# One Trainium2 core: a layer of sliding attention and a gated feed-forward, with the order of its steps replaced

## Chip, core and metric

The kernel runs on one core of one Trainium2 chip. The metric is the device time of one execution in microseconds (us), as the median of several runs. Engines are named as the profile names them: PE is TensorE, DVE is VectorE, ACT is ScalarE, POOL is GpSimd and SP is SyncE, which here only starts transfers.

## What is computed

Two blocks follow each other on 2048 tokens of 512 values in bfloat16. The first is attention with 32 heads of 16 values, in which each token looks at itself and seven earlier ones, two apart. The second is a gated feed-forward of width 1376. Each has a layer norm ahead of it and its input added behind it.

```python
def _A_ref(x, wqkv, wo):                      # H = 32, Dh = 16, W = 8, dil = 2
    qkv = (x @ wqkv).reshape(B, S, 3, H, Dh).transpose(2, 0, 3, 1, 4)
    q, k, v = qkv[0], qkv[1], qkv[2]
    idx = pos[:, None] - (jnp.arange(W) * dil)[None, :]
    mask = idx >= 0
    logits = jnp.einsum("bhsd,bhswd->bhsw", q, kg) * Dh ** -0.5   # kg, vg: k, v gathered at idx
    attn = softmax(jnp.where(mask, logits, -1e9))
    o = jnp.einsum("bhsw,bhswd->bhsd", attn, vg)
    return o.transpose(0, 2, 1, 3).reshape(B, S, D) @ wo

def _B_ref(x, W_gate, W_up, W_down):
    gate = x @ W_gate
    return ((gate * (gate > 0)) * (x @ W_up)) @ W_down

h = x + _A_ref(_layernorm(x), A_wqkv, A_wo)
out = h + _B_ref(_layernorm(h), B_W_gate, B_W_up, B_W_down)
```

## The kernel before

The tokens are cut into four chunks of 512 (tk 0 to 3 in the code, here the first to the fourth chunk). Each chunk goes through the same steps, and the chunks overlap:

- Layer norm: statistics on DVE (L467, L470), the scale on ACT (L480, L484), the normalised rows into a tile "row" (L515 on DVE, L512 on ACT). The rows are then transposed into a "quad" tile, either on PE (L544) with a copy out by ACT or DVE (L558, L560), or by DMA transposes that SP starts (L533).
- Query, key and value projections on PE (L585) and copies out by ACT (L593). In the first chunk the projections are cut into small column pieces, so that PE can begin when the first 128 tokens are normalised.
- Scores: DVE multiplies the query by shifted keys (L636, L651), in one case pairs are added, and PE sums over a head's values with a 32 column selection matrix (L642, L694). ACT takes the exponential (L708), PE sums it per head (L725), ACT inverts that, and DVE scales the exponentials (L752).
- The weights are then broadcast over a head's values by DMA, from tile "ex" into tile "big" (L768), four transfers of 128 KB for each half of the window, started by SP or by POOL.
- DVE multiplies them by the shifted values (L800). The eight products are summed by an accumulating DMA of 512 KB that POOL starts (L843), and the rest by DVE (L803, L837).
- Output projection on PE (L881). DVE adds the input (L892), ACT squares for the second norm (L457), DVE writes the centred rows (L510), and SP transposes them by DMA (L533).
- Gate and up on PE (L954; the last 96 columns at L921). ACT copies them out, into tile "up_sb" (L958) and tile "gr" (L961), and DVE multiplies them into "gT" (L982). There are two up_sb buffers.
- Down projection on PE (L1005). For the third and fourth chunk DVE scales it and adds the residual (L1013), and SP stores it (L1019). For the first and second chunk ACT scales it into up_sb (L1011), POOL adds that to x_sm by an accumulating DMA (L1034), and SP stores x_sm (L1037). Until that addition has landed the up_sb buffer is not free.

All results of PE go into eight "bank" tiles.

What sets the order is a list of numbers. The code first writes down all steps (add, class Plan), with the engine, what each depends on, what buffers it takes, and a duration and latency for the planner. RANK gives every step a place. With RANK the planner takes the steps strictly by it and gives each the buffer that by its own reckoning comes free first; each engine then has its steps in that order, and runs them strictly one after another. Only this line of it matters here:

```python
            for op in (waiting[-1:] if RANK else waiting):
```

Constants such as SW, PEL, AL and DL are the planner's latencies. They issue nothing. The first steps (setup) are not in the list: the loads of the input and of the attention weights, the load of the gate weights, and the constants.

Of the kernel before, what the change touches and what calls it, by code (L numbers as in the profile page):

```python
# [8 lines left out]
P = 128  # L9
# [192 lines left out]
def kernel(  # L202
# [103 lines left out]
    def f_load(n, i):  # L306
        if n == "d":
            lo, hi = (0, 5) if i == 0 else (5, NFF)
            nc.sync.dma_start(
                wd_sb[:, lo:hi, :], B_W_down[lo * P:hi * P, :].rearrange("(ft p) n -> p ft n", p=P))  # L310
            if FTAIL and i:
                nc.sync.dma_start(wd_sb[:FTAIL, NFF, :], B_W_down[NFF * P:F, :])
        else:
            w = B_W_up.rearrange("(dt p) f -> p dt f", p=P)
            nc.sync.dma_start(wgu_sb[:, 2 * i:2 * i + 2, 1, :], w[:, 2 * i:2 * i + 2, :])

    def setup():
# [31 lines left out]
        nc.sync.dma_start(wgu_sb[:, :, 0, :], B_W_gate.rearrange("(dt p) f -> p dt f", p=P))  # L349

# [40 lines left out]

    BCN = 4
# [4 lines left out]
    TMT = (0, 1, 2, 3)  # L397
    TTM, DTG, ATE = 0.0825, 0.27, 0.225
# [6 lines left out]
    SW = 0.21  # L405
    PEL = 0.22
    A5, A10, AX, AS = 0.48, 0.9, 0.713, 0.2
    AL = 0.13
    D2, D5, D10, D20, D40, DST, DSM = 0.335, 0.665, 0.603, 1.135, 2.202, 0.595, 0.08
    DXN = 0.33  # L410
    DL = 0.12
# [18 lines left out]
    fills = [add(("warm", 0), "PE", 5.6, f_warm, [], -500, take=[wb])]  # L430

# [8 lines left out]
    def layernorm(tk, src, dst_slots, pr, groups, on_act, residual=None):  # L440
# [7 lines left out]
        for grp in groups:  # L448
# [78 lines left out]
            for j0 in range(lo, hi, step):  # L527
# [24 lines left out]
                tev = not residual and tk == 0 and j0 == 1  # L552
# [15 lines left out]
    for tk in range(NCK):  # L568
# [52 lines left out]
        kp = {t: kdone.get((tk - 1, t)) for t in range(NT)}  # L621
        for hf in range(2):
# [55 lines left out]
            elif (tk, hf) in PRE:  # L678
# [19 lines left out]
                scd = [add(("sc%d" % hf, tk), "PE", nu * MM + SW, f_sc, [a], apr, take=[sc], use=[prd[0][1]], lat=PEL)]  # L698
# [8 lines left out]
            def f_ex(sc=sc, ex=ex):  # L707
                nc.scalar.activation(out=ex.t[:], in_=sc.t[:], func=ACT.Exp, scale=SCALE)  # L708

            def f_mk(hf=hf, ex=ex):  # L710
                V.tensor_tensor(out=ex.t[:, 0:PADL], in0=ex.t[:, 0:PADL], in1=mask[:, hf, :],
                                op=ALU.mult)

            a = add(("ex%d" % hf, tk), "ACT", A5, f_ex, scd, apr, take=[ex], use=[sc], lat=AL)
            if tk == 0:
                a = add(("mk%d" % hf, tk), "DVE", DSM, f_mk, [a], apr, use=[ex], lat=DL)
            exs.append(ex)
            exd.append(a)


        dn, rc = Buf(at_s), Buf(rc_s)

        def f_dn(exs=exs, dn=dn, tk=tk, es=None):
# [371 lines left out]
```

## Time and profile before

| what | value |
|---|---|
| three runs | 191.80, 192.64 and 192.98 us; median 192.64 us |
| span of the profiled execution, from first to last instruction | 190.2 us |
| granted TensorE clock, mean | 0.998 |
| HBM read, written | 8.42 MB, 2.10 MB |

The profile is of one execution. Its page gives the span; a time of that execution beside the span is not given, and the median of the runs is 2.4 us above the span. Times in the profile count from the span's first instruction. A row of the grouped view has line, engine, operation, output and input tiles, shapes and count, then busy time, mean ns of one, and idle time before. A row of the timeline has start, length, engine, line, operation, tiles and count, and in brackets the engine's idle time before it with what ended that. SPq is SP's queue; its length there is the time to start the transfers, not to move them.

### The profile page before, as it was taken

Reading aid. Unit: us, or ns where it says so; the run is one execution under the profiler, and the core shown is the slowest. Engines: PE = TensorE matmul, PEld = TensorE weight load, DVE = VectorE, ACT = ScalarE, POOL = GpSimd, SP = SyncE. Lnnn points to the kernel's source line nnn. Section 1 sums busy time; section 2 is a strip of 40 time slices with the busy share of each in tenths; the row PEclk is TensorE's granted clock in tenths of the full one; section 3 lists DMA queues with packets and bytes.
Section 4 is the critical chain, followed back from the end, with each engine's and each line's share of the span. In section 5 each row is a group of like instructions: output and inputs, shape, how many; then the busy total and the mean of one; then the engine's idle time right before and its main releaser. Section 6 shows DMA issues by size and latency. Waiting matters only on the chain.

```text
span 190.2 us, 3080 instructions
## 1 busy us (share of the span) xinstructions
PE 185.1 (97%) x1127; PEld 95.4 (50%) x1127; DVE 150.7 (79%) x231; ACT 113.5 (60%) x234; POOL 25.2 (13%) x47
## 2 busy tenths in 40 slices
PE   7799999999999999999999999999999999999993
PEld 7676555554444445544344464444454444455453
DVE  5899999999999999999999998998485712114324
ACT  2579999985467945762483795146466713358500
POOL 4000221400000004230033123027000000000000
PEclk9999999999999999999999999999999999999999
DMA  5999364993198858998438798779922211000503
GB/s 182 281 347 370 90 163 87 191 194 59 21 330 177 233 166 153 194 191 182 83 65 152 142 181 186 180 137 166 221 44 55 55 28 59 28 0 0 165 3 110
DMA packets 27743, 26.98 MB, mean 142 GB/s; under 512 B 14704, under 2 KB 23248, under 8 KB 27728
## 3 DMA queue, kind: packets, MB, share of 16 engines
q1 hardware_dynamic: 23696, 15.34, 29.7%
q0 software_dynamic: 3312, 10.49, 28.6%
q10 hardware_dynamic: 720, 0.95, 1.5%
q8 instruction: 9, 0.15, 0.3%
q14 instruction: 6, 0.05, 0.1%
HBM read 8.42 MB, written 2.10 MB: 55 GB/s over the span
## 4 chain that ended last, share of the span: by engine, by line
PE 82%; ACT 11%; DMA 3%; DVE 1%; issue 1%; SPq 0%
PE bank L954 37%; PE bank L1005 20%; PE bank L585 12%; PE bank L881 7%; ACT row L512 5%; DMA x_sm<-in_A_x_dram 3%; PE bank L921 3%; ACT quad L560 2%; ACT vT L593 2%; PE bank L642 2%; ACT quad L593 1%; PE bank L694 1%; ACT kT L593 1%; ACT ex L708 1%; SPq L323 0%
## 5 line engine op out<-in xcount | busy, mean ns | idle before, releaser
L954 PE MATMUL bank<-quad,wgu_sb 128*128 128x512 bf16 x320 | 72.3, 379 | 0.0
L954 PEld LDWEIGHTS <-wgu_sb 128*128 128x128 bf16 x320 | 30.9, 98 | 37.3 <-issue 1.7
L1005 PE MATMUL bank<-wd_sb,gT 128*128 128x512 bf16 (+3 forms) x198 | 39.7, 355 | 0.0
L958 ACT CAST up_sb<-bank 128x512 bf16<-128x512 f32 x40 | 23.1, 591 | 21.0 <-PE bank L954 14.9
L585 PE MATMUL bank<-quad,wqk_sb 128*128 128x512 bf16 (+2 forms) x176 | 30.4, 321 | 0.5 <-DVE quad L558 0.4
L961 ACT ACTIVATE gr<-bank 128x512 bf16<-128x512 f32 x40 | 23.3, 606 | 9.7 <-PE bank L954 8.2
L1005 PEld LDWEIGHTS <-gT 128*128 128x128 bf16 (+1 forms) x198 | 18.5, 98 | 19.7
L982 DVE TENSOR_TENSOR gT<-gr,up_sb 128x1024 bf16<-128x1024 bf16 x20 | 13.6, 686 | 14.4 <-PE bank L1005 7.0
L636 DVE TENSOR_TENSOR big<-quad,kT 128x4096 bf16<-128x4096 bf16 x11 | 24.8, 2279 | 0.0
L585 PEld LDWEIGHTS <-wqk_sb 128*128 128x128 bf16 x176 | 17.1, 113 | 11.4 <-issue 1.1
L800 DVE TENSOR_TENSOR big<-big,vT 128x4096 bf16<-128x4096 bf16 x9 | 20.4, 2281 | 0.0
L843 POOL DMA_DIRECT2D big<-big x13 | 11.6, 965 | 64.3 <-PE bank L954 32.6
L1013 DVE SCALAR_TENSOR_TENSOR row<-bank,iv,x_sm 128x512 bf16<-128x512 f32 (+2 forms) x10 | 6.3, 643 | 13.4 <-PE bank L1005 13.2
L457 ACT ACTIVATE junk<-x_sm,sm 128x512 bf16<-128x512 bf16 x16 | 11.6, 727 | 8.8 <-DVE x_sm L892 8.8
L585 PE MATMUL bank<-quad,wv_sb 128*128 128x512 bf16 x64 | 16.1, 380 | 0.2 <-ACT quad L560 0.2
L881 PE MATMUL bank<-wo_sb,quad 128*128 128x512 bf16 x64 | 15.0, 379 | 0.0
L892 DVE SCALAR_TENSOR_TENSOR x_sm<-x_sm,bank 128x512 bf16<-128x512 bf16 x16 | 10.8, 678 | 2.4 <-PE bank L881 2.4
L803 DVE TENSOR_TENSOR big<-big 128x1024 bf16<-128x1024 bf16 (+1 forms) x17 | 10.3, 622 | 1.6 <-DMA big<-big 1.4
L467 DVE BATCH_NORM_STATS2 st<-x_sm 128x6 f32<-128x512 bf16 x16 | 10.2, 679 | 1.1 <-DMA x_sm<-in_A_x_dram 1.1
L593 ACT CAST quad<-bank 128x512 bf16<-128x512 f32 x16 | 9.3, 594 | 2.5 <-PE bank L585 2.4
L593 ACT CAST kT<-bank 128x512 bf16<-128x512 f32 x16 | 9.3, 596 | 1.9 <-PE bank L585 1.0
L593 ACT CAST vT<-bank 128x512 bf16<-128x512 f32 x16 | 9.1, 610 | 2.1 <-PE bank L585 2.1
(80 smaller groups left out, 175.6 us busy)
## 6 DMA issues: line engine op xcount, KB each, us to landing
big<-big POOLq DMA_DIRECT2D x13, 512.0 KB, 5.2
big<-ex SPq DMA_DIRECT2D x20, 128.0 KB, 3.1
big<-ex POOLq DMA_DIRECT2D x12, 128.0 KB, 3.8
wgu_sb<-in_B_W_gate_dram SPq DMA_DIRECT2D x1, 1376.0 KB, 9.3
wgu_sb<-in_B_W_up_dram SPq DMA_DIRECT2D x2, 688.0 KB, 5.0
wd_sb<-in_B_W_down_dram SPq DMA_DIRECT2D x2, 640.0 KB, 5.7
x_sm<-in_A_x_dram SPq DMA_DIRECT2D x2, 512.0 KB, 6.2
wqk_sb<-wqk_sb POOLq DMA_DIRECT2D x2, 512.0 KB, 5.8
```

What stands on the lines that cost most here:

```text
L457: nc.scalar.activation(out=junk[:, j % 2, :], in_=h.t[:] if h else x_sm[:, tk * BPC + j, :], func=ACT.Square, bias=sm.t[:, j:j + 1], scale ...
L585: nc.tensor.matmul(mm.t[:, lo:hi], lhsT=wv_sb[:, dt, t:D:NT] if c == 2 else wqk_sb[:, dt, c * D + t:(c + 1) * D:NT], rhs=xnT.t[:, dt, lo:h ...
L593: nc.scalar.copy(out=o, in_=mm.t[:])
L636: V.tensor_tensor(out=pb.t[:].rearrange("p (t w) s -> p t w s", t=2), in0=q4, in1=k4, op=ALU.mult)
L800: V.tensor_tensor(out=mt.t[:], in0=ab.t[:], in1=v8, op=ALU.mult)
L843: nc.gpsimd.dma_start(mt.t[:, 0:4, :], mt.t[:, 4:8, :], accum_op=ALU.add)
L881: nc.tensor.matmul(od.t[:], lhsT=OT.t[:, t, j * P:(j + 1) * P], rhs=wo_sb[:, t, :], start=(t == 0), stop=(t == NT - 1 and tk not in RPE))
L954: nc.tensor.matmul(mm.t[:fs, lo:hi], lhsT=wgu_sb[:, dt, g, ft * P: ft * P + fs], rhs=hnT.t[:, dt, lo:hi], start=(dt == 0), stop=(dt == NT ...
L958: nc.scalar.copy(out=ub.t[:fs, i, :], in_=um.t[:fs, :])
L961: nc.scalar.activation(out=gr.t[:fs, i, :], in_=gm.t[:fs, :], func=ACT.Relu)
L982: V.tensor_tensor(out=gt.t[:fs, 0:n, :], in0=gr.t[:fs, 0:n, :], in1=ub.t[:fs, 0:n, :], op=ALU.mult)
L1005: nc.tensor.matmul(od.t[:, c0:c1], lhsT=gts[ft].t[:fs, ft % 2, j * P:(j + 1) * P], rhs=wd_sb[:fs, ft, c0:c1], start=(ft == 0), stop=(ft == ...
```

## The change

The table RANK is replaced by another one of the same 745 numbers. Of the old and the new one the first row:

```diff
 RANK = [
-    0, 1, 2, 3, 4, 5, 6, 7, 8, 9, 18, 10, 11, 12, 14, 15, 16, 17, 13, 19,
...
+    1, 0, 2, 4, 5, 6, 8, 9, 11, 12, 10, 7, 3, 13, 14, 15, 16, 17, 18, 21,
...
 ]
```

Four planner latencies change, and three switches are added, each at the value that keeps the program's steps as they were: MS is empty, TEV holds the tile that was written out before, and the gate weights would be loaded later only if LATE, which stays "ud", held a "g".

```diff
+        elif n == "g":
+            nc.sync.dma_start(wgu_sb[:, :, 0, :], B_W_gate.rearrange("(dt p) f -> p dt f", p=P))
...
-        nc.sync.dma_start(wgu_sb[:, :, 0, :], B_W_gate.rearrange("(dt p) f -> p dt f", p=P))
-
+        if "g" not in LATE:
+            f_load("g", 0)
...
+    MS = ()
...
+    TEV = (1,)
...
-    SW = 0.21
-    PEL = 0.22
+    SW = 0.19
+    PEL = 0.15
...
-    AL = 0.13
+    AL = 0.1
...
-    DL = 0.12
+    DL = 0.1
...
-                tev = not residual and tk == 0 and j0 == 1
+                tev = not residual and tk == 0 and j0 in TEV
...
-                scd = [add(("sc%d" % hf, tk), "PE", nu * MM + SW, f_sc, [a], apr, take=[sc], use=[prd[0][1]], lat=PEL)]
+                if tk in MS:
+                    both.append((sc, ex, [a], [prd[0][1]], nu, f_sc))
+                else:
+                    scd = [add(("sc%d" % hf, tk), "PE", nu * MM + SW, f_sc, [a], apr, take=[sc], use=[prd[0][1]], lat=PEL)]
+            elif tk in MS:
+                both.append((sc, ex, [a for a, _, _ in prd], [b for _, b, _ in prd], 4, lambda p=prd: [f() for _, _, f in p]))
...
-            for n in LATE:
+            for n in LATE.replace("g", ""):
```

Every engine has the same instructions in another order. In what follows a row is the line, the operation, the tile written and the tiles read (the number behind a name tells tiles of one kind apart), the shape and the count. Lines after the change are 2 to 23 higher: L475 was L467, L523 was L515, L566 was L558, L775 was L752, L791 was L768, L541 was L533, L963 was L940, L1057 was L1034, L866 was L843.

The first place is DVE's start: statistics (BN_STATS, BN_AGGR) of the first chunk's four row tiles, their normalised rows row_104 to row_107, and the copy of one transposed tile into quad. Before:

```order
L467 BN_STATS st_114<-x_sm 128x6
L470 BN_AGGR mv_117<-st_114 128x2
L515 TENSOR_SCALAR row_104<-x_sm,mv_117,rs_129 128x512
L467 BN_STATS st_115<-x_sm 128x6
L515 TENSOR_SCALAR row_105<-x_sm,mv_117,rs_129 128x512
L470 BN_AGGR mv_117<-st_115 128x2
L467 BN_STATS st_116<-x_sm 128x6
L470 BN_AGGR mv_117<-st_116 128x2
L558 COPY quad_79<-bank_140 128x4x128
L515 TENSOR_SCALAR row_106<-x_sm,mv_117,rs_129 128x512
```

After the change:

```order
L475 BN_STATS st_114<-x_sm 128x6
L478 BN_AGGR mv_117<-st_114 128x2
L523 TENSOR_SCALAR row_104<-x_sm,mv_117,rs_129 128x512
L475 BN_STATS st_115<-x_sm 128x6
L523 TENSOR_SCALAR row_105<-x_sm,mv_117,rs_129 128x512
L478 BN_AGGR mv_117<-st_115 128x2
L566 COPY quad_79<-bank_139 128x4x128
L475 BN_STATS st_116<-x_sm 128x6
L478 BN_AGGR mv_117<-st_116 128x2
L523 TENSOR_SCALAR row_106<-x_sm,mv_117,rs_129 128x512
```

The copy has moved ahead of the fourth tile's statistics. The first two tiles have also changed places: row_104 now holds the second 128 tokens, which the copy belongs to, and row_105 the first.

The second place is where the third chunk's attention ends and the fourth chunk's weights (ex_100 and ex_102) are scaled. On DVE before:

```order
L752 TENSOR_TENSOR ex_102<-ex_102,rec_103 128x512
L803 TENSOR_TENSOR wqk_sb<-wqk_sb 128x1024
L931 TENSOR_TENSOR row_108<-gr_112,bank_142 128x2x96
L837 TENSOR_TENSOR quad_83<-big_90 128x512
L837 TENSOR_TENSOR quad_83<-wqk_sb 128x512
L803 TENSOR_TENSOR big_89<-big_89 128x1024
L837 TENSOR_TENSOR quad_83<-big_89 128x512
```

After:

```order
L826 TENSOR_TENSOR wqk_sb<-wqk_sb 128x1024
L775 TENSOR_TENSOR ex_100<-ex_100,rec_103 128x512
L860 TENSOR_TENSOR quad_82<-wqk_sb 128x512
L826 TENSOR_TENSOR big_91<-big_91 128x1024
L860 TENSOR_TENSOR quad_82<-big_91 128x512
L775 TENSOR_TENSOR ex_102<-ex_102,rec_103 128x512
L915 SCALAR_TENSOR_TENSOR x_sm,sm_121<-x_sm,bank_141 128x512
```

The scaling of ex_102 has moved behind the last of the attention's output rows (quad). On SP, at the same place, the broadcast that reads ex_102 and the transposes of the third chunk's normalised rows (into quad_86), before:

```order
L768 DMA big_88<-ex_102 128x1x512 x4
L1037 DMA out_dram<-x_sm 128x2x512
L940 DMA_TRANSPOSE gT_97<-row_108 128x4x128
L533 DMA_TRANSPOSE quad_86<-row_107 128x4x128
L533 DMA_TRANSPOSE quad_86<-row_104 128x4x128
L533 DMA_TRANSPOSE quad_86<-row_105 128x4x128
L533 DMA_TRANSPOSE quad_86<-row_106 128x4x128
```

After:

```order
L963 DMA_TRANSPOSE gT_96<-row_108 128x4x128
L791 DMA big_89<-ex_102 128x1x512 x4
L541 DMA_TRANSPOSE quad_86<-row_104 128x4x128
L541 DMA_TRANSPOSE quad_86<-row_106 128x4x128
L541 DMA_TRANSPOSE quad_86<-row_105 128x4x128
L541 DMA_TRANSPOSE quad_86<-row_107 128x4x128
```

A store has gone from between them and the transpose of the second chunk's last feed-forward columns (gT) now stands ahead of the broadcast.

The third place is POOL's list around the first chunk's residual additions (x_sm from up_sb) and the third chunk's accumulations (big, wqk_sb). Before:

```order
L768 DMA big_91<-ex_102 128x1x512 x4
L1034 DMA x_sm<-up_sb_109 128x1024
L1034 DMA x_sm<-up_sb_110 128x1024
L843 DMA big_92<-big_92 128x2048
L843 DMA wqk_sb<-wqk_sb 128x2048
L843 DMA big_90<-big_90 128x2048
L843 DMA big_89<-big_89 128x2048
```

After:

```order
L791 DMA big_92<-ex_101 128x1x512 x4
L1057 DMA x_sm<-up_sb_110 128x1024
L866 DMA big_90<-big_90 128x2048
L866 DMA big_88<-big_88 128x2048
L1057 DMA x_sm<-up_sb_109 128x1024
L866 DMA wqk_sb<-wqk_sb 128x2048
L866 DMA big_91<-big_91 128x2048
```

Two accumulations now stand between the two additions.

More of the change, by code (lines that the diff above doesn't have):

```diff
@@ L430 @@
     fills = [add(("warm", 0), "PE", 5.6, f_warm, [], -500, take=[wb])]
+    if "g" in LATE:
+        wload["g"].append(add(("ldg", 0), "SP", 0.45, lambda: f_load("g", 0), wload["o"], 0, lat=1.0, dq=(1.0, 3.6)))
     def fill(d, k):
@@ L621 @@
         kp = {t: kdone.get((tk - 1, t)) for t in range(NT)}
+        both = []
         for hf in range(2):
@@ L705, with f_ex, f_mk @@
                                    take=[sc], use=[pb], lat=PEL))
[L707 to L718, printed above, removed]
+            if tk in MS and hf == 0:
+                continue
+            if tk in MS:
+                a = add(("sc1", tk), "PE", sum(x[4] for x in both) * MM + SW, lambda p=both: [x[5]() for x in p],
+                        [d for x in both for d in x[2]], apr, take=[x[0] for x in both], use=[d for x in both for d in x[3]], lat=PEL)
+                scs = [(h, x[0], x[1], [a]) for h, x in enumerate(both)]
+            else:
+                scs = [(hf, sc, ex, scd)]
+            for h, sc, ex, scd in scs:
+                def f_ex(sc=sc, ex=ex):
+                    nc.scalar.activation(out=ex.t[:], in_=sc.t[:], func=ACT.Exp, scale=SCALE)
+                def f_mk(h=h, ex=ex):
+                    V.tensor_tensor(out=ex.t[:, 0:PADL], in0=ex.t[:, 0:PADL], in1=mask[:, h, :],
+                                    op=ALU.mult)
+                a = add(("ex%d" % h, tk), "ACT", A5, f_ex, scd, apr, take=[ex], use=[sc], lat=AL)
+                if tk == 0:
+                    a = add(("mk%d" % h, tk), "DVE", DSM, f_mk, [a], apr, use=[ex], lat=DL)
+                exs.append(ex)
+                exd.append(a)
         dn, rc = Buf(at_s), Buf(rc_s)
```

74 rows, old and new, of the table RANK are left out of this document.

## The prediction

> **What bounds the kernel now.** I read the page's first two parts, then the busy time by stretches, what TensorE waited for, and the chain of waits. Part 1 of the page, with busy time and share of the span:
>
> ```profile
> span 190.2 us, 3080 instructions
> PE 185.1 (97%) x1127; PEld 95.4 (50%) x1127; DVE 150.7 (79%) x231; ACT 113.5 (60%) x234; POOL 25.2 (13%) x47
> ```
>
> TensorE (PE) is idle 190.2 - 185.1 = 5.1 us. The stretches say where (start:end, length, then each engine's busy time):
>
> ```profile
> 0.00:10.50 10.50, 8.48 (x128) 7.75 (x129) 7.82 (x29) 4.89 (x12) 1.91 (x16) 1.00 0.76 234
> 10.50:40.00 29.50, 29.34 (x210) 17.30 (x210) 29.27 (x48) 27.88 (x52) 5.90 (x8) 1.00 0.75 204
> 40.00:70.00 30.00, 30.00 (x180) 13.82 (x178) 30.00 (x36) 19.49 (x40) 0.00 (x0) 1.00 0.69 176
> ...
> 187.30:190.20 2.90, 0.00 (x0) 0.00 (x0) 0.35 (x1) 0.00 (x0) 0.00 (x0) 0.89 0.34 97
> ```
>
> About 2.0 us lie before 10.5, 0.2 before 40, 2.9 in the tail. TensorE's waits (total, times, longest) are all of the first two:
>
> ```profile
> PE bank L428 <- DVE warm L327: 1.0, 1, 1.0
> PE bank L544 <- DVE row L515: 0.5, 1, 0.5
> PE bank L585 <- DVE quad L558: 0.4, 1, 0.4
> PE bank L585 <- ACT quad L560: 0.2, 1, 0.2
> ```
>
> The 1.0 us stands before the first matmul of all, behind a memset in the setup, which the change leaves alone. The tail is the last output slice's arithmetic and store. So waits that another order can take away sum to 0.5 + 0.4 + 0.2 = 1.1 us. Is busy time at full pace? Two pieces of the chain of waits (start, length, what):
>
> ```profile
> 59.27 8.63 PE bank L954 x40
> ...
> 177.72 9.59 PE bank L1005 x66
> ```
>
> 40 matmuls in 8.63 us are 216 ns each at 512 columns; the granted clock is 1.00 in all stretches but the tail. From 40 to 187.3 TensorE is full and already at its pace: in nearly the whole span a new order has nothing to win there and can only open holes.
>
> **The change part by part.** Every engine keeps its instructions; each runs its own list in order, so what counts is where TensorE's next operand is now later or earlier than its turn. The added code paths are not entered (MS is empty, LATE is "ud", TEV holds the old value 1): no cost. The changed planner constants issue nothing; with ranks given they reach the program through which free buffer is taken.
>
> *Head.* The row order of VectorE is in the section on the change. TensorE, VectorE (DVE) and ScalarE in the first 10 us, by the timeline (start, length, what, idle time before and its end):
>
> ```profile
> 5.77 0.40 PE L544 MATMUL bank<-identity,row 128*128 128x128 bf16 x4
> 6.69 0.40 PE L544 MATMUL bank<-identity,row 128*128 128x128 bf16 x4 [0.52 <-DVE row L515]
> 7.37 0.83 PE L585 MATMUL bank<-quad,wqk_sb 128*128 128x128 bf16 x12
> 8.60 0.27 PE L585 MATMUL bank<-quad,wqk_sb 128*128 128x128 bf16 x2 [0.40 <-DVE quad L558]
> ...
> 7.33 0.69 DVE L467 BATCH_NORM_STATS2 st<-x_sm 128x6 f32<-128x512 bf16 x1 [0.61 <-DMA x_sm<-in_A_x_dram]
> 8.15 0.39 DVE L558 COPY quad<-bank 128x512 bf16<-128x512 bf16 x1
> 8.46 0.79 DVE L515 TENSOR_SCALAR row<-x_sm,mv,rs 128x512 bf16<-128x512 bf16 x2
> ...
> 6.21 0.58 ACT L560 COPY quad<-bank 128x512 bf16<-128x512 bf16 x1 [0.23 <-PE bank L544]
> ```
>
> Before, the copy of the second tile (DVE, 8.15) stands behind the fourth tile's statistics, which wait 0.61 us for a load; TensorE waits 0.40 us for that copy. Now that tile is transposed first (near 5.7, done by 6.2), and its copy fits into VectorE's idle 0.61 us, done by 7.1: the 0.40 us wait goes. What is late next: the other tile, whose transposes keep the second turn (6.69 + 0.40 = 7.09, minus 0.1), is copied by ScalarE in 0.58 us, so the first projection matmuls go at about 7.65 instead of 7.37, a new wait of 0.3 us. The third tile's normalisation (8.46) moves up by the copy's 0.39 less 0.1 of overlap, to 8.16, and with it its transposes by 0.3. Both paths then meet the fourth tile, whose load lands as before. Net between 0 and -0.4 us; I take -0.3, since the third tile's turn is what TensorE meets last.
>
> *Projections and scores, 10.5 to 40.* TensorE's one wait is 0.2 us. The same load feeds it; between -0.2 (it goes) and +0.3 (a second one like it): 0.
>
> *Transposes of the third chunk.* The four DMA transposes of the normalised rows feed its gate/up matmuls. SyncE (SP), TensorE and VectorE there, with the two uncrowded broadcasts near 57 us and the landing range of the transposes at the end:
>
> ```profile
> 57.48 5.11 SPq L768 DMA_DIRECT2D big<-ex  x8
> 114.75 3.94 SPq L768 DMA_DIRECT2D big<-ex  x4
> 118.78 0.55 SPq L1037 DMA_DIRECT2D out_dram<-x_sm  x1
> 119.43 1.26 SPq L940 DMA_TRANSPOSE gT<-row  x1
> 120.79 5.15 SPq L533 DMA_TRANSPOSE quad<-row  x4
> ...
> 117.73 3.62 PE L881 MATMUL bank<-wo_sb,quad 128*128 128x512 bf16 x16
> 121.19 6.22 PE L1005 MATMUL bank<-wd_sb,gT 128*128 128x512 bf16 x28
> 127.31 2.97 PE L954 MATMUL bank<-quad,wgu_sb 128*128 128x512 bf16 x13
> ...
> 114.25 0.42 DVE L752 TENSOR_TENSOR ex<-ex,rec 128x512 bf16<-128x512 bf16 x1
> 116.84 0.43 DVE L837 TENSOR_TENSOR quad<-big 128x512 bf16<-128x512 bf16 x1
> ...
> DMA to landing us min/median/max: 2.4/2.5/5.2
> ```
>
> Before, the last transpose leaves near 124.7 and lands 2.5 us later, 127.2: just in time for the gate/up matmuls at 127.31. Now the product on which the broadcast waits (L752, 0.42 us) stands behind the last output row of the attention (L837) on VectorE, so it starts near 117 and SyncE's broadcast near 117.3; the four transposes are queued right behind it. The broadcast took 3.94 us beside GpSimd's own broadcasts, and 5.11 / 2 = 2.55 us without them. So the transposes start at 119.9 to 121.2. Four at 1.22 us (the last leaves 3.7 us after the first) and 2.5 us to land: 126.1 to 127.4. The same matmuls stand ahead of TensorE's gate/up in both orders (16, then 28), so its turn is 127.3 less the head's 0.3 = 127.0. It waits 0 to 0.4 us; the broadcasts of GpSimd are still beside it, so the upper row is nearer, and with the 0.1 us that a landing needs to release TensorE I take +0.5. The broadcast's reader, the fourth chunk's multiplication, comes later with it; TensorE's gate/up work of the third chunk, queued by then, hides that, and without the cover it would cost the broadcast's own shift, 117.3 - 114.75 = 2.5 us.
>
> By the Trainium skill (DMA: Bandwidth & Descriptors, Issuing engines are not separate DMA queues), transfers started by different engines run on the same 16 DMA engines and interleave, and a second issuer saves only issue time. That speaks against this place: by it the broadcast keeps the 3.94 us, without it 2.55 and the term is 0; the two rows (3.94 against 2.55) agree with it.
>
> *Accumulations on GpSimd (POOL).* Its list now puts two 512 KB accumulations between the two residual additions that release the up_sb buffers. Rows: its issues near 98 us, what ScalarE waited for, landing, and queue 0:
>
> ```profile
> 95.21 0.91 POOL L1034 DMA_DIRECT2D x_sm<-up_sb  x1 [12.55 <-ACT up_sb L1011]
> 98.23 0.86 POOL L1034 DMA_DIRECT2D x_sm<-up_sb  x1 [2.11 <-ACT up_sb L1011]
> 100.83 0.85 POOL L843 DMA_DIRECT2D big<-big  x1 [1.73 <-DVE big L800]
> ...
> ACT up_sb L958 <- DMA x_sm<-up_sb: 2.6, 2, 2.4
> ...
> big<-big POOLq DMA_DIRECT2D x13, 512.0 KB, 5.2
> x_sm<-up_sb POOLq DMA_DIRECT2D x4, 256.0 KB, 3.3
> ...
> q0 software_dynamic: 3312, 10.49, 28.6%
> ```
>
> Queue 0 was busy 28.6% of 190.2 = 54.4 us for 10.49 MB, so 0.52 MB cost about 2.7 us (an estimate from that row). Two ahead put the second addition's landing from 98.2 + 3.3 = 101.5 to at most 101.5 + 5.4 = 107. Before, ScalarE waited 2.4 us for it and TensorE did not, the eight banks covering that. Now ScalarE's next four copies, two pairs, go into the other buffer, which the first addition frees (before: 95.2 + 3.3 = 98.5), and the fifth needs this one. A pair goes with gate and up of two tiles on TensorE, 16 matmuls or 3.5 us; two pairs put the fifth near 98.5 + 7 = 105.5 or later. I take 0; if the cover is short it costs the 1.5 us from there to 107, more below.
>
> *Everything else.* SyncE sends one transpose between the two 688 KB loads of the first chunk instead of behind both; the stores move later, and nothing reads them. The last down projection still ends the program with the same two quarter slices. 0 each.
>
> Sum: -0.3 + 0 + 0.5 + 0 = +0.2 us on the profiled execution. Its span is 190.2; the median of the three runs is 192.64, 2.4 us more, and the page doesn't give the profiled execution's own time apart from its span, so I put the same 2.4 around it: 192.64 + 0.2, rounded 192.9.
>
> **The rivals.**
>
> (a) *The residual addition holds ScalarE* (slower). If the accumulations ahead land like the slowest of them, the second addition comes later still. The row:
>
> ```profile
> DMA to landing us min/median/max: 4.5/5.2/10.3
> ```
>
> 10.3 against 5.2 is 5.1 us; past 107 the fifth copy waits and the banks fill; the 2.4 us that ScalarE waited before without stopping TensorE are the cover. So it decides from a landing of about 105.5 + 2.4 = 108 on and costs up to 107 + 5.1 - 108 = 4 us, in the middle +2: with the sum, 194.9. For: GpSimd's list says it; against: only one of thirteen need have taken that long. Chance 0.10.
>
> (b) *The third chunk's transposes land late* (slower). With the longest landing of 5.2 us instead of 2.5, TensorE waits 2.7 us more, 195.6. For: before had no slack here (127.2 against 127.31), and now nothing stands between the broadcast and them. Against: the median is 2.5, and the 5.2 was in another chunk, behind the large loads. Chance 0.08.
>
> (c) *All short waits go* (0.5 + 0.4 + 0.2) and no new one comes: -1.1, 191.5. Against: two of them hang on loads that don't move. Chance 0.06.
>
> (d) *TensorE is not full.* Its busy 72.3 us for 320 matmuls hold more than 320 x 0.216 = 69.1:
>
> ```profile
> L954 PE MATMUL bank<-quad,wgu_sb 128*128 128x512 bf16 x320 | 72.3, 379 | 0.0
> ```
>
> 3.2 us, if they were holes and not the ends of pipelined matmuls, would give 189.4. Against: the 216 ns of the chain's pieces. Chance 0.03. The Trainium skill (Perfetto Trace Analysis, Identifying the Most-Contended Engine) holds the busy share of matmuls for a poor measure of what is left and names the share of weight loads, here 50%; the trace does not bear that out as room for an order, since no weight load ended a wait of TensorE in the rows above.
>
> (e) *The order's text changes but not what waits*: that is the forecast within 0.3 us, and counted with it.
>
> **How the numbers follow.** Forecast 0.73, (a) 0.10, (b) 0.08, (c) 0.06, (d) 0.03. The forecast's own range is 191.8 to 193.8: -0.4 - 0.2 and +0.3 + 0.4 for its terms, and the runs' own spread of about 0.6 either way. (c) takes the low end to 191.5. Above, taking in the middle of (a) and leaving out (b) gives 194.9. One per cent, 1.9 us, is about what a measurement of this kernel can tell from no change: below 190.7 lies (d) with a sixth of (c), for the runs' spread, 0.04; above 194.6 lie (a) and (b), 0.18; 0.78 is between.
>
> **What would show it.** Right: VectorE's copy (L566) before 7.1 and no wait on it; a TensorE wait of 0.3 to 0.7 us on a transpose near 127; span 190 to 191. Wrong: a TensorE wait on ScalarE between 100 and 112 with x_sm<-up_sb behind it (a); transposes of the third chunk landing after 128 (b); TensorE idle below 4.2 us in all (c), (d); or waits of TensorE at places that I have put at 0.

## The result and the profile after

| kernel | median, us | runs | span of the profiled execution, us |
|---|---|---|---|
| before | 192.22 (191.43 to 192.98) | 4 | 190.2 |
| after | 194.09 (193.81 to 194.33) | 4 | 192.6 |

After against before is a ratio of 1.0102, with a 95% interval of [1.0061, 1.0142]: about 1.9 us slower by the medians and 2.4 us by the spans, which are of one execution each (that of after is the slowest of its four). The forecast was 192.9 us, +0.2. The time lies outside the forecast's own range (191.8 to 193.8) and inside the whole one (191.5 to 194.9), whose upper part was put there for rival (a). The sum missed most of the loss.

Part 1 of the page after, span and busy time:

```profile
span 192.6 us, 3057 instructions
PE 184.4 (96%) x1108; PEld 95.6 (50%) x1127; DVE 150.5 (78%) x231; ACT 113.7 (59%) x234; POOL 25.2 (13%) x47
```

1108 matmuls are recorded instead of 1127. The 19 missing records leave short gaps that are no waits: matmuls start every 216 ns and their records are 379 ns long, so one missing record leaves 432 - 379 = 53 ns, and PE's busy time is too small by about 1 us in all (an estimate from these figures). TensorE's waits show better (total, times, longest; the first six of seven, the seventh is of 0.2 us):

```profile
PE bank L977 <- issue: 1.3, 1, 1.3
PE bank L433 <- DVE warm L329: 1.0, 1, 1.0
PE bank L944 <- ACT up_sb L981: 0.9, 1, 0.9
PE bank L977 <- DMA quad<-row: 0.3, 1, 0.3
PE bank L593 <- ACT quad L568: 0.2, 1, 0.2
PE bank L552 <- DVE row L523: 0.2, 1, 0.2
```

The 1.0 us behind the memset is as before. Where the three new ones stand, by the timeline of TensorE (start, length, what, idle time before and its end), with the score sums ahead of the first:

```profile
93.89 0.61 PE L703 MATMUL bank<-big,sel 128*32 128x512 bf16 x8
95.82 2.53 PE L977 MATMUL bank<-quad,wgu_sb 128*128 128x512 bf16 x11 [1.32 <-issue]
...
128.71 1.67 PE L977 MATMUL bank<-quad,wgu_sb 128*128 128x512 bf16 x7 [0.31 <-DMA quad<-row]
...
141.84 0.82 PE L944 MATMUL bank<-wgu_sb,quad 128*128 128x192 bf16 x8 [0.89 <-ACT up_sb L981]
```

In the kernel before the first two places read so:

```profile
94.21 0.62 PE L694 MATMUL bank<-big,sel 128*32 128x512 bf16 x8
94.83 2.53 PE L954 MATMUL bank<-quad,wgu_sb 128*128 128x512 bf16 x11
...
127.31 2.97 PE L954 MATMUL bank<-quad,wgu_sb 128*128 128x512 bf16 x13
```

The score sums at 94 start 0.3 us earlier than before, and then TensorE loses 1.32 + 0.31 + 0.89 = 2.5 us. -0.3 + 2.5 = +2.2 of the 2.4 us of span. Only the middle one of the three waits was in the forecast.

**The stall at 94.5.** TensorE has to begin the second chunk's gate/up product, whose operand comes from four DMA transposes. SyncE's queue before:

```profile
81.70 4.18 SPq L768 DMA_DIRECT2D big<-ex  x4
85.98 1.26 SPq L940 DMA_TRANSPOSE gT<-row  x1
88.33 5.12 SPq L533 DMA_TRANSPOSE quad<-row  x4
```

The four transposes of before by line (fastest, median and slowest in ns, first and last start), and their landings:

```profile
L533 SPq DMA_TRANSPOSE quad<-row x4: 1191/1206/1216, 88.3 to 92.3; - x4
...
DMA to landing us min/median/max: 2.4/2.4/2.5
```

The last left at 92.3 and landed 2.4 to 2.5 us later, near 94.7, against matmuls that began at 94.83: this place had no slack before the change. SyncE's queue after:

```profile
82.33 1.63 SPq L963 DMA_TRANSPOSE gT<-row  x1
84.01 4.43 SPq L791 DMA_DIRECT2D big<-ex  x4
88.55 5.90 SPq L541 DMA_TRANSPOSE quad<-row  x4
```

The single transpose (of the first chunk's last feed-forward columns) and the broadcast (of the third chunk's first weights) have changed places. Before, SyncE was done with both at 85.98 + 1.26 = 87.24 and then idle for 1.1 us until the first normalised row was written. Now the broadcast ends at 84.01 + 4.43 = 88.44 with no idle time left, and the first of the four transposes alone takes 1.96 us (their fastest is 1.21). The same two rows of after:

```profile
L541 SPq DMA_TRANSPOSE quad<-row x4: 1211/1222/1961, 88.5 to 93.2; - x4
...
DMA to landing us min/median/max: 2.4/2.5/3.3
```

The last leaves at 93.2 and needs 2.5: 95.7, against TensorE's turn at 93.89 + 0.61 = 94.5. Of the 1.0 us by which SyncE is done later than before (94.45 against 93.45), 0.2 is the later start and 0.8 the slow first transpose. The slowness does not need a full queue: in e2, e4 and e8 below, SyncE was idle for 0.2 to 0.5 us between the broadcast and the four transposes, these still took 6.11, 6.24 and 6.27 us, and TensorE waited 1.06 to 1.22 us.

**The stall at 141.** TensorE waits for a bank that ScalarE has not emptied. ScalarE and GpSimd (POOL) in that stretch, after:

```profile
126.20 0.67 ACT L1034 ACTIVATE up_sb<-bank,iv 128x512 bf16<-128x512 f32 x1
...
135.44 0.68 ACT L1034 ACTIVATE up_sb<-bank,iv 128x512 bf16<-128x512 f32 x1
...
141.21 1.07 ACT L981 CAST up_sb<-bank 128x512 bf16<-128x512 f32 x2 [2.70 <-DMA x_sm<-up_sb]
...
127.34 0.91 POOL L866 DMA_DIRECT2D big<-big  x1 [7.72 <-DVE big L823]
129.54 0.87 POOL L866 DMA_DIRECT2D big<-big  x1 [1.29 <-DVE big L823]
131.74 0.85 POOL L866 DMA_DIRECT2D big<-big  x1 [1.32 <-DVE big L823]
136.41 0.85 POOL L1057 DMA_DIRECT2D x_sm<-up_sb  x1 [3.82 <-ACT up_sb L1034]
```

The kernel before, same engines:

```profile
126.20 1.84 ACT L1011 ACTIVATE up_sb<-bank,iv 128x512 bf16<-128x512 f32 x3 [3.87 <-PE bank L1005]
...
125.47 0.91 POOL L843 DMA_DIRECT2D big<-big  x1 [9.25 <-DVE big L800]
128.34 0.87 POOL L1034 DMA_DIRECT2D x_sm<-up_sb  x1 [1.96 <-ACT up_sb L1011]
```

The up_sb buffer holds two tiles of the second chunk's down projection until their residual addition has landed. Before, ScalarE scaled three of its tiles in one go, and the first addition left at 128.34. Now the second tile of the pair is scaled 9 us behind the first, the addition leaves at 136.41 and needs 4.7 us, and ScalarE stands for 2.70 us at a copy that wants this buffer.

### The profile page after: what moved, and what is told of

Read it like the earlier page. It is cut to its first block, busy times and chain, and to the rows that moved or that the text cites. A ratio compares the mean times of both kernels' runs of the same rounds, so it can differ in the third digit from the quotient of the medians.

```text
span 192.6 us, 3057 instructions
## 1 busy us (share of the span) xinstructions
PE 184.4 (96%) x1108; PEld 95.6 (50%) x1127; DVE 150.5 (78%) x231; ACT 113.7 (59%) x234; POOL 25.2 (13%) x47
## 4 chain that ended last, share of the span: by engine, by line
PE 55%; DVE 16%; issue 13%; DMA 11%; POOL 3%; ACT 1%; SPq 0%; POOLq 0%; DVEq 0%; ACTq 0%
PE bank L977 28%; PE bank L1028 15%; DVE big L660 4%; DMA big<-big 4%; PE bank L593 4%; DMA x_sm<-in_A_x_dram 4%; DVE big L838 4%; PE bank L904 4%; DVE st L475 3%; PE bank L944 3%; DMA x_sm<-up_sb 2%; DVE big L645 2%; POOL big L866 2%; PE bank L651 1%; POOL big L791 1%
## 5 line engine op out<-in xcount | busy, mean ns | idle before, releaser
L1028 PE MATMUL bank<-wd_sb,gT 128*128 128x512 bf16 (+4 forms) x193 | 40.0, 355 | 0.3
L981 ACT CAST up_sb<-bank 128x512 bf16<-128x512 f32 x40 | 22.6, 592 | 25.3 <-PE bank L977 17.4
L984 ACT ACTIVATE gr<-bank 128x512 bf16<-128x512 f32 x40 | 22.8, 604 | 12.3 <-PE bank L977 6.6
L593 PE MATMUL bank<-quad,wqk_sb 128*128 128x512 bf16 (+2 forms) x172 | 29.6, 320 | 0.4 <-ACT quad L568 0.2
L866 POOL DMA_DIRECT2D big<-big x13 | 11.6, 894 | 32.9 <-DVE big L823 24.5
L791 POOL DMA_DIRECT2D big<-ex x12 | 6.8, 589 | 31.5 <-DVE ex L734 20.2
L475 DVE BATCH_NORM_STATS2 st<-x_sm 128x6 f32<-128x512 bf16 x16 | 10.3, 680 | 0.5 <-DMA x_sm<-in_A_x_dram 0.4
L593 PEld LDWEIGHTS <-wv_sb 128*128 128x128 bf16 x64 | 7.0, 114 | 6.3 <-issue 1.0
```

Source lines behind the costliest of these rows:

```text
L475: V.bn_stats(out=st.t[:], in_=x_sm[:, tk * BPC + j, :])
L593: nc.tensor.matmul(mm.t[:, lo:hi], lhsT=wv_sb[:, dt, t:D:NT] if c == 2 else wqk_sb[:, dt, c * D + t:(c + 1) * D:NT], rhs=xnT.t[:, dt, lo:h ...
L866: nc.gpsimd.dma_start(mt.t[:, 0:4, :], mt.t[:, 4:8, :], accum_op=ALU.add)
L981: nc.scalar.copy(out=ub.t[:fs, i, :], in_=um.t[:fs, :])
L984: nc.scalar.activation(out=gr.t[:fs, i, :], in_=gm.t[:fs, :], func=ACT.Relu)
L1028: nc.tensor.matmul(od.t[:, c0:c1], lhsT=gts[ft].t[:fs, ft % 2, j * P:(j + 1) * P], rhs=wd_sb[:fs, ft, c0:c1], start=(ft == 0), stop=(ft == ...
```

## The experiments

All but e8 and e9 move single steps in the list of the changed kernel (e6 does so in the kernel before), behind a named other step, with everything else and all buffers as they are. Each set of runs had its own runs of the kernel before, with medians of 192.02 us (e1, e2, e4, e5; 29 runs), 192.01 (e3, e6, e7, e8; 29) and 191.98 (e9; 11); the ratios of e1 to e9 are to these, that of after is to 192.22. A span is of one execution, whose time lies up to 0.7 us from the median of its version (e9); the ratios, not the spans, say what a version is worth. The waits are those in brackets on TensorE's timeline, or "-" where it has none of over 0.2 us.

| run | median, us | ratio to before, 95% interval | span | waits near 95 / 128 / 141 |
|---|---|---|---|---|
| after | 194.09 | 1.0102 [1.0061, 1.0142] | 192.6 | 1.32 / 0.31 / 0.89 |
| e1 broadcast first | 193.31 | 1.007 [1.004, 1.01] | 191.0 | - / 0.53 / 0.25 |
| e2 addition early | 193.28 | 1.0061 [1.0036, 1.0085] | 191.4 | 1.06 / 0.28 / - |
| e3 scaled early | 193.26 | 1.0065 [1.0038, 1.0092] | 191.8 | 1.31 / 0.27 / - |
| e4 fourth chunk's scaling early | 194.38 | 1.0106 [1.007, 1.0143] | 192.6 | 1.19 / 0.48 / 1.1 |
| e7 e1 and e2 | 192.43 | 1.0018 [0.9993, 1.0043] | 190.5 | - / 0.51 / - |
| e5 e1, e2 and e4 | 192.18 | 1.0005 [0.9982, 1.0028] | 190.1 | - / - / - |
| e6 kernel before, swapped | 192.41 | 1.0022 [0.9989, 1.0056] | 191.3 | 0.67 / - / - |
| e8 14 memsets | 194.00 | 1.0103 [1.0061, 1.0145] | 192.1 | 1.2 / 0.3 / 0.7 |
| e9 40 memsets | 194.89 | 1.0136 [1.0093, 1.0179] | 193.8 | 1.24 / 0.9 / 0.7 |

**e1: the broadcast ahead of the transpose again.** The numbers are places in the code's own list of steps; 218 is the single transpose on SyncE (first chunk), 462 the broadcast (third chunk's first weights; the expectations of e6 to e8 call it the second chunk's, as it stands ahead of that chunk's four transposes).

```diff
     todo = plan.order()
+    for a, b in ((218, 462),):
+        op = next(o for o in todo if o.seq == a)
+        todo.remove(op)
+        todo.insert(1 + next(i for i, o in enumerate(todo) if o.seq == b), op)
```

> The changed kernel with one step moved on SyncE: the transpose of the first chunk's last feed-forward columns goes back behind the broadcast of the third chunk's first weights, as before the change. Theory (SyncE's order): in the changed kernel TensorE stood still 1.4 us near 94 us for the second chunk's transposes, which left SyncE only at 88.55 because that transpose (1.63 us) was ahead of the broadcast (84.01 to 88.4). The broadcast should now start near 82.1 and end near 86.5, the four transposes start near 88.1 and land by 94.3: the stall falls from 1.4 to under 0.4 us, and span and time fall by about 1.0 us (192.6 to 191.6; ratio to before about 1.005). Rival (the broadcast itself is slow beside GpSimd's own broadcast, whatever stands ahead): transposes still land after 95.4, no change of the span beyond 0.3 us. Second rival (the gain is given back): the stall near 94 goes, but the wait for the up_sb buffer near 140 grows from 1.05 to about 2 us, span unchanged.

SyncE's queue in e1:

```profile
82.16 3.05 SPq L791 DMA_DIRECT2D big<-ex  x4
85.31 1.29 SPq L963 DMA_TRANSPOSE gT<-row  x1
88.17 5.12 SPq L541 DMA_TRANSPOSE quad<-row  x4
```

The broadcast goes 1.85 us sooner than after, so its data were ready and it had only stood behind the transpose. SyncE is idle again for 1.6 us ahead of the four transposes, these take 5.12 us as before, and TensorE's wait at 95 is gone. This is the theory of SyncE's order; neither rival shows. The span falls by 1.6 us: 1.32 for this wait and 0.6 at 141, less 0.2 that is added at 128. The median falls by 0.8 us only; the profiled execution of e1 was one of its faster ones.

**e2: scaling and addition early.** ScalarE's scaling of the pair's second tile (391) goes right behind the down projection on TensorE that it reads (390), so that on ScalarE it follows the first tile's scaling again, and GpSimd's addition (392) ahead of the second and third accumulation.

```diff
+    for a, b in ((391, 390), (392, 632)):
```

> The changed kernel with two steps moved: ScalarE's scaling of the second chunk's second output rows goes right behind the first (from 135.4 to about 127 us), and GpSimd's residual addition that reads both goes behind one of the fourth chunk's accumulations instead of three. Theory (up_sb held): TensorE's stall of 1.05 us near 141 us is a bank that ScalarE could not empty, since its copy waited 2.7 us for the addition's landing at 141.1; with the addition out near 128.5 it lands by 134, the wait and the stall go, span -1.0 us (192.6 to 191.6). Rival (the accumulations, now pushed behind the addition, become late and the fourth chunk's output projection waits): the stall at 141 goes but TensorE waits 0.5 us or more on VectorE or a landing between 142 and 152, span changed by less than 0.5 us.

GpSimd in e2:

```profile
126.89 0.91 POOL L866 DMA_DIRECT2D big<-big  x1 [7.37 <-DVE big L823]
128.02 0.87 POOL L1057 DMA_DIRECT2D x_sm<-up_sb  x1 [0.21 <-issue]
129.09 0.85 POOL L866 DMA_DIRECT2D big<-big  x1 [0.20 <-issue]
131.29 0.84 POOL L866 DMA_DIRECT2D big<-big  x1 [1.35 <-DVE big L823]
```

The addition leaves 8.4 us sooner, ScalarE no longer waits for it, TensorE's wait at 141 is gone, and the span falls by 1.2 us (the median by 0.8), as the theory had it.

**e3: the scaling alone.** GpSimd's list stays as in after, so that ScalarE's lateness and the accumulations ahead in GpSimd's list are told apart. The addition spoken of is the one at 136.41.

```diff
+    for a, b in ((391, 390),):
```

> The changed kernel with one move: on ScalarE the second chunk's second output scaling (its residual rows) goes right behind the row it stood behind in the kernel before; GpSimd's list stays, with the three accumulations ahead of that chunk's second residual addition. Theory one (ScalarE's late scaling is what makes the addition late): the addition is issued right behind the third accumulation, near 132.6 us instead of 136.4, lands near 137 to 139 instead of 141.1, ScalarE waits under 1 us for up_sb there, TensorE's 0.9 us wait behind ScalarE's L981 goes, and the span is 191.5 to 191.9 us instead of 192.6 (ratio to the kernel before near 1.006). Theory two (the accumulations ahead in GpSimd's queue are what makes it late): the addition still lands at 140 or later, TensorE's wait of 0.9 us stays within 0.2, and the span is 192.3 to 192.8 (ratio near 1.010).

GpSimd and ScalarE in e3:

```profile
131.65 0.85 POOL L866 DMA_DIRECT2D big<-big  x1 [1.32 <-DVE big L823]
132.18 1.19 POOL L1057 DMA_DIRECT2D x_sm<-up_sb  x1
...
139.18 1.56 ACT L981 CAST up_sb<-bank 128x512 bf16<-128x512 f32 x3 [0.98 <-DMA x_sm<-up_sb]
```

Theory one holds: the addition goes right behind the third accumulation, lands near 139.1, and TensorE's wait is gone. The accumulations ahead cost the addition some 4 us of waiting (132.18 against 128.02 in e2), which ScalarE's remaining wait of 0.98 us shows and TensorE does not feel. What made it 2 us too late was ScalarE.

**e4: the scaling on VectorE ahead of the third chunk's transposes early** (of the fourth chunk's second weights; the step that the forecast's +0.5 rested on), 628 back behind 627.

```diff
+    for a, b in ((628, 627),):
```

> The changed kernel with one step moved on VectorE: the scaling of the fourth chunk's second weights goes from behind the third chunk's last attention rows to right behind the first scaling (118.6 to about 116.7 us). Theory (the term of the prediction): SyncE's broadcast then starts near 117.2 instead of 119.04, takes up to 3.9 us beside GpSimd's, the four transposes of the third chunk start by 121.1 instead of 122.09 and TensorE's wait of 0.4 us near 128.4 goes: span -0.3 to -0.4 us, which the times can hardly tell; the profile can. Rival (VectorE's work ahead of the output projection is late by the 0.4 us that was moved ahead of it): the output projection of the third chunk waits 0.3 us or more, no gain.

SyncE's queue at that place, first after, then e4:

```profile
119.04 2.95 SPq L791 DMA_DIRECT2D big<-ex  x4
122.09 5.22 SPq L541 DMA_TRANSPOSE quad<-row  x4
```

```profile
116.83 3.80 SPq L791 DMA_DIRECT2D big<-ex  x4
120.72 6.39 SPq L541 DMA_TRANSPOSE quad<-row  x4
```

The broadcast starts 2.2 us earlier, and the end of the four transposes moves from 127.31 to 127.11: 0.2 us. The rest is given back, since the broadcast now runs beside GpSimd's own (in e4 from 117.01 to 119.24) and takes 3.80 instead of 2.95, and the transposes take 6.39 instead of 5.22. TensorE waits 0.48 us. A miss: by itself the edit gains nothing that can be measured.

**e7 and e5: two and three moves together.**

```diff
+    for a, b in ((218, 462), (391, 390), (392, 632)):
```

```diff
+    for a, b in ((218, 462), (391, 390), (392, 632), (628, 627)):
```

> The changed kernel with SyncE's second-chunk broadcast put ahead of the transpose again, and with the second chunk's second residual addition early again (ScalarE's scaling and GpSimd's addition), but without the third chunk's scaling put back on VectorE. If the two losses are separate and all there is beside the third chunk's transposes, the span is 190.4 to 190.8, TensorE's only waits beyond the head are 0.3 to 0.7 us near 127, and the ratio is 1.001 to 1.004. If undoing the two only moves the loss to the third chunk's transposes, TensorE waits 1 us or more there, and the ratio is 1.006 or above, so that the third chunk's move is needed for the rest.

> The changed kernel with the three moves together (SyncE's broadcast ahead of the feed-forward transpose, the residual addition early, the scaling early). Theory (three separate stalls, which add): span 192.6 - 1.0 - 1.0 - 0.4 = 190.1 us, the time that of the kernel before within 0.4% (ratio 0.997 to 1.002). Rival (TensorE's stalls are one chain, and what one gives the next takes): the span stays above 191, ratio above 1.004. If the head's 0.3 us and all three stalls go, it is faster than the kernel before by 0.1 to 0.4 us.

TensorE's waits in e5:

```profile
PE bank L433 <- DVE warm L329: 1.0, 1, 1.0
PE bank L593 <- ACT quad L568: 0.2, 1, 0.2
```

Two moves take 2.1 us off the span, three 2.5 (1.7 and 1.9 off the median, against 0.8 for each of e1 and e2 alone), and with three the kernel is at the time of before (1.0005). Both came as expected for separate losses. So the loss is two places that add up, and the third chunk's transposes are what is left: 0.51 us in e7. In e5 that wait is gone too: SyncE starts the four transposes at 120.11 instead of 121.12, though the broadcast ahead of them takes 3.57 us instead of 2.56. The times of e7 and e5 can't tell this 0.4 us, as their ratios overlap. No version here beats the kernel before.

**e6: the kernel before with SyncE's pair swapped**, the order alone without the rest of the change.

```diff
+    for a, b in ((462, 218),):
```

> The kernel before with one move on SyncE: the second chunk's broadcast goes behind the single transpose of gT instead of ahead of it, which is the order of the changed kernel at that place. If that pair's order alone costs the time, TensorE waits 1 to 1.4 us near 95 us and the span is 191.2 to 191.6 instead of 190.2 (ratio near 1.006). If the order costs only together with what else the changed kernel does there (GpSimd's broadcast started in the same time), the broadcast takes about 4 us, TensorE waits 0 to 0.5 us, and the span is 190.2 to 190.7 (ratio 1.000 to 1.003).

SyncE's queue in e6, and TensorE's turn:

```profile
82.84 2.36 SPq L940 DMA_TRANSPOSE gT<-row  x1
85.25 4.07 SPq L768 DMA_DIRECT2D big<-ex  x4
89.43 5.16 SPq L533 DMA_TRANSPOSE quad<-row  x4
...
95.97 1.24 PE L954 MATMUL bank<-quad,wgu_sb 128*128 128x512 bf16 x5 [0.67 <-issue]
```

A miss of both: the wait of 0.67 us lies between the two expectations, and the time (1.0022, interval across 1) tells nothing. By this one profile the order costs about half of the 1.32 us by itself. The single transpose (2.36 us) and the broadcast (4.07) are slow here, and none of the four transposes is. GpSimd's own broadcast went out from 81.05 to 83.28, beside the single transpose but 2 us ahead of SyncE's broadcast; why that is slow all the same was not tried.

**e8 and e9: GpSimd's broadcast later**, SyncE untouched. In after GpSimd starts its own broadcast at 84.15, SyncE at 84.01. Memsets into a constant that is no longer read delay it.

```diff
+    NPAD = 14        # e9: 40
...
+            if op.seq == 463:
+                for _ in range(NPAD):
+                    nc.gpsimd.memset(warm[:], 0.0)
```

> The changed kernel with 14 small memsets on GpSimd ahead of its own broadcast of the second chunk, so that it is issued 2 to 3 us later than 84.15 us; SyncE's list is untouched. Theory one (the broadcasts of two engines slow one another, and the four transposes behind them): SyncE's broadcast takes 2.6 to 3.2 us instead of 4.43 and the first of the four transposes about 1.2 instead of 1.96, the wait of TensorE near 95 us falls from 1.3 to below 0.4, and the span falls to 191.3 to 191.8 (ratio near 1.004). Theory two (only the order on SyncE counts, one transfer after the other): the broadcast takes 4 us or more, TensorE's wait near 95 stays at 1.2 or above, and the span stays at 192.4 to 192.8.

> As in the run with 14 memsets, now 40 of them (about 10 us by the 3.08 us that 12 took), since the 14 fitted into GpSimd's idle time and moved its broadcast by nothing (83.98 us). GpSimd's broadcast of the second chunk should now be issued near 87 to 88 us, behind SyncE's. Theory one (the two broadcasts slow one another): SyncE's broadcast takes 2.6 to 3.2 us instead of 4.43, TensorE's wait near 95 us falls from 1.3 to below 0.5, and the span falls to 191.3 to 191.9 us, provided that the GpSimd broadcast's own reader on VectorE is not late; the transposes may still be slowed by it, first one included. Theory two (SyncE's order alone): the broadcast takes 4 us or more and TensorE's wait near 95 stays at 1.2 or above.

e8 tells nothing: GpSimd had 6.5 us to spare, the memsets fitted in, and the broadcast went at 83.98. In e9 it went at 89.14; SyncE's queue and GpSimd's:

```profile
84.60 2.54 SPq L792 DMA_DIRECT2D big<-ex  x4
88.80 6.06 SPq L542 DMA_TRANSPOSE quad<-row  x4
...
89.14 2.23 POOL L792 DMA_DIRECT2D big<-ex  x4 [0.23 <-issue]
```

The four transposes of e9 by line (fastest, median and slowest in ns, first and last start):

```profile
L542 SPq DMA_TRANSPOSE quad<-row x4: 1190/1230/2037, 88.8 to 93.6; - x4
```

The broadcast takes 2.54 us, in the same place of SyncE's queue, instead of the 3.78 to 4.43 us of the five versions in which GpSimd's goes out beside it (after, e2, e3, e4, e8): that GpSimd's broadcast makes it slow there is shown. It is done 1.7 us ahead of the transposes. But TensorE's wait stays, 1.24 us: GpSimd's broadcast now runs beside the four transposes, one of which takes 2.04 us instead of 1.2, and they land up to 5.9 us after their issue instead of up to 3.3. The expected fall of the wait did not come: the delay followed the broadcast. The time of e9 is no measure of that place, since its later broadcast also holds VectorE, and other waits grow.

## Why the prediction was right and wrong

- **The head, -0.3: right.** VectorE's copy runs at 6.57 and nothing waits on it; ScalarE's copy of the other tile now ends a wait of 0.23 us, the new one of 0.3 that was worked out, and the first projection matmuls go at 7.70 (forecast 7.65). The score sums near 94 are 0.3 us earlier. The same order gives 93.64 to 94.84 for these in the nine profiled runs of it, mean 94.0, and the old order 94.21 and 94.68 in its two; so the sign is likely, the size not settled.
- **Projections and scores, 0: right.** No wait above 0.2 us there.
- **The third chunk's transposes, +0.5: the place and the reason right, the size in part by luck.** TensorE waits 0.31 us in after (forecast 0 to 0.4, taken as 0.5), and 0.51 to 0.53 where the stall at 94.5 is undone (e7, e1). Two errors cancel in it: the broadcast started at 119.04, not 117.3, and took 2.95 us, not 3.94. VectorE's late scaling (118.55 in after) had put it behind most of GpSimd's broadcast (117.39 to 119.62); this is not an effect of the stall, since in e1, without it, the broadcast stands wholly behind GpSimd's (116.23 to 118.46, then 118.56) and takes 2.54. So the nearer row was the lower one, 2.55. That VectorE's late scaling causes the wait is borne out by e5 against e7, though not in after by itself (e4), where the earlier broadcast meets GpSimd's and the end moves by 0.2 us.
- **"Everything else ... 0 each" failed.** This is the step that missed the larger half. The pair on SyncE ahead of the second chunk's transposes, single transpose and broadcast, was among it, and was left out of the working; it cost TensorE 1.3 us (e1 takes that wait away). ScalarE's later scaling of the second chunk, 0.9 us on TensorE, was among it too (e3 takes it away). The working for the third chunk names most of what was needed, transposes queued behind a broadcast that is slowed beside GpSimd's; it was not done for each chunk. What it doesn't have is that the first of those transposes can be slow too, 1.96 us in after instead of the 1.22 that it takes for each, which is 0.8 of the 1.0 us by which SyncE is late there. The rule cited there from the Trainium skill (DMA: Bandwidth & Descriptors, Issuing engines are not separate DMA queues), that transfers of different issuers share the same 16 DMA engines, speaks against this place as well, and the runs agree that the two are not independent: SyncE's broadcast takes 4.43 us to start beside GpSimd's (after), 2.54 without (e9).
- **"Accumulations on GpSimd ... I take 0": right at its place.** The first chunk's second addition went out at 98.83 and landed 7.7 us later, at 106.5 (forecast: 107 at most), and ScalarE did not wait for it. ScalarE waits for an addition once in after, at 141. Rival (a), a residual addition that holds ScalarE through up_sb and so TensorE, is what happened, but to the second chunk's addition, and not by GpSimd's queue, which (a) took for its cause, but by ScalarE's own late scaling (e3). Its price of +2 was for another place; here it is 0.9 us on TensorE.
- **Rival (b)** was not it, though the sign named for it came: the third chunk's last transpose landed at 128.6, after 128, because it left late (126.1), not because it landed slowly (2.5 us; the slowest of the four took 3.3). TensorE's wait there is 0.3 us, not 2.7. **(c) and (d)** fell: waits grew. That TensorE has no reserve is borne out by e5, in which nearly all waits are gone and the span is 190.1 us, as before.
- **The signs.** The copy ahead of 7.1 and the wait near 127 came. The span of 190 to 191 did not, and the sign named for that, "waits of TensorE at places that I have put at 0", did.
- **The chances and the range.** The ratio of 1.0102 stands at the bound between within 1% and slower. Its bounds in time for 0.78, 190.7 to 194.6, hold the measured 194.09, but 0.78 was too much: it took in no chance of a new wait at a place left out of the working, of which there were two. Luck helped the number. The forecast stands on a median of 192.64 us for the kernel before, while its larger sets of runs give 192.0, so it was 0.6 us nearer to the result than its +0.2 deserved; and the whole range reaches to 194.9 only for rival (a) at another place. The range of the forecast itself, 191.8 to 193.8, is narrower than its terms as they are added up there: 192.9 - 0.6 - 0.6 to 192.9 + 0.7 + 0.6 is 191.7 to 194.2.

How e1's move also eased the wait at 141 (0.25 instead of 0.89) was not tried apart. By the traces TensorE's turn there came 0.9 us earlier, and the addition went out 0.9 us earlier (135.47) and landed in 4.1 us instead of 4.7; why it landed faster stays open, as does why the first of the four transposes at 88 is slow.

## What to carry to other kernels

Where one engine is full, a new order costs there what it takes beyond the slack of that engine's operands. List for every chunk, not for one, when the last transfer lands against that engine's turn (0.1 us ahead of it at 94.8 here), the idle time of the queue before it, and what now stands ahead of it in the queue. A buffer that is filled in two parts is held from the first part to the landing behind the second: look at the gap between the parts, on the engine that fills it, before the queue that empties it. And an order that moves a transfer out of one collision may move it into the next (e4, e9), so undo single moves and read the queue rows, not the sum.

## What was not expected of the hardware

- A broadcast of four transfers of 128 KB leaves SyncE in 2.54 us where GpSimd's is not beside it (e9; also 2.54 right behind GpSimd's, at 118.56 in e1), in 2.85 to 3.05 us where GpSimd's begins 2 us after it (e1, e5, e7, near 82), and in 3.57 to 4.43 us where both begin within 0.4 us of each other (after, e2, e3, e4, e8; e5 at 116) or GpSimd's a little over 1 us ahead (before: 4.18 and 3.94). It is the issue on SyncE that gets longer, so all that is queued behind shifts. The 4.07 us of e6, where GpSimd had issued its own 2 us before, don't fit this.
- DMA transposes can be slow as well. In after, e2, e3, e4 and e8 the first of the four transposes near 88 takes 1.96 to 2.34 us and the other three about 1.2; in e9, beside GpSimd's broadcast, the third takes 2.04. But being queued right behind a broadcast isn't enough: the first transposes at 122.09 in after (1.29 us) and at 89.43 in e6 (1.23) are not slow.
- A residual addition of 256 KB landed 3.3 us after its issue at the fastest in e2 and e3, 6.9 us in e3 right behind the third of three accumulations, and 7.8 us at the slowest in both, for the first chunk's second addition, which follows two accumulations.
